# Hash-masked attention before two gated layers: split q and k in place, three fills a head, one matmul for the shift row

## Chip, cores and metric

One core of a Trainium2 chip runs the whole program in one launch. The metric is device time in microseconds. A profiled execution gives a span (first to last instruction of the program) and a time that is a little longer; the times of plain runs compare with the latter.

## The reference, cut to what matters

```python
# q, k, v: (2, 8, 768, 64); proj: (64, 6)
q_bucket = sum(((q @ proj) > 0) * 2 ** arange(6))          # k_bucket alike
mask = q_bucket[:, :, :, None] == k_bucket[:, :, None, :]
scores = where(mask, q @ k.T / 8, -1e9)
attn = exp(scores - max(scores)); attn = attn / (sum(attn) + 1e-9)
x = (attn @ v) as (2, 768, 512)                            # heads side by side
# layer 1: gate = sigmoid(causal 5-tap convolution of x), per channel
x = (gate * (x @ w_val)) @ w_out
# layer 2: token shift, xk and xr are mixes of x and the row before it
k = relu(xk @ w_k); y = (k * k) @ w_v
out = sigmoid(xr @ w_r) * y
```

## The kernel before

**Numbers in two halves.** Products keep float32 accuracy by splitting each factor into a high half (rounded to the matmul type) and the rest (low half). Keys lie along partitions in the score matmuls: a head's q tile and k tile have 128 partitions and two planes of 768 columns. In `scores` (L329, L330) the first matmul multiplies plane 1 and the second plane 0, both over 128 partitions, into one PSUM bank of 128 keys by 384 queries. Plane 0 holds 64 rows of the high half and a block of 32 rows that makes the mask: bits of the hash, which give a large negative number where q and k fall into different buckets, and one row with the negative row maximum of each query (the shift). Plane 1 holds cross terms of high and low halves.

**Before smax and scores.** Heads go in pairs. `load_q` and `load_k` fetch a pair, `turn` transposes on TensorE into PSUM, `turn_out` (ACT) copies to `t32`. `split_hi` (L445, ACT) writes the rounded half of a pair to `hlq` or `hlk`, `split_lo` (L449, VectorE) the rest. Then `fill` moves each head's halves from there to the head's tiles by four transfers on SP's queue (L468 and L470 of 384 KB, L472 and L474 of 192 KB), and `penalty` (L479, L482) moves the bits of `bits_gt` and `bits_big` there, both heads of a pair in one transfer of 96 KB. The tiles of two pairs take turns, in the memory named `big`.

**A head.** `smax` (L355) computes plane 0 products of a block of 128 queries with all keys, `smax_row` (L359, VectorE) takes the maximum, `smax_all` (L363) negates it. `shift` (L368) turns the six columns of maxima into a row: six matmuls with a one-column factor, each of 128 columns. `shift_row` (L374, ACT) copies that row of 768 to its place in plane 0. Then per block of 128 keys and half of the queries: `scores`, `exp` (L334, ACT) into a ring of 11 buffers, `add` (L338, GpSimd) for the sums, and `values` (L343, four matmuls for a block of keys). `sums`, `sums_fold` (L391, a small transfer to `dn`), `spread`, `spread_out` (L406, a small transfer to `rb`) and `norm` (L410) give the quotient, and `norm_out` writes the head to `xT`.

**Weights.** Each of 28 weight tiles is loaded (`weight`, L600), converted in two passes on ACT (L583, L586) and two on VectorE (L590, L594), and split by `part_hi` (ACT) and `part_lo` (VectorE for a list of tiles, else GpSimd). The order is val, out, k, r, v: 20 tiles have memory of their own, and the eight of v pass through three late buffers. The gated layers (all matmuls L648) run in four chunks of 384 tokens; the first ones begin between the last heads.

**Order.** The program text has a hand-over list, `ORDER`: some 2300 events such as `sc201` (`scores`, head 2, block 0, half 1), which fixes the order on every engine and on SP's queue at once. Each engine works its own instructions strictly in this order. All transfers of this stage are issued by SP in this order; before it issues one, SP waits for what the transfer reads and overwrites.

Of the kernel before, what the change touches and what calls it, by code (L numbers as in the profile page):

```python
# [11 lines left out]
R = mybir.dt.float32r  # L12
# [8 lines left out]
NRING = 11  # L21
# [23 lines left out]
fl ze00 ze01 ft01 ft00 fy01 fh01 lv0 ve0 fy00 lq10 lk1 lq11 we00 ve1 fc fb00 fb01 fz00 fz01 fb11 fg wa0 ft10 wa2 wa8  # L45
wa7 ft11 fy11 fb10 fz10 fy10 sb fh10 fh00 wa4 fh11 ve2 sm00 fz11 sr00 sm01 fo00 fo01 sx sr01 sz se0 fo02 fo03 sm02
tu100 sr02 sm03 to100 sr03 sm04 se1 fo10 wa5 sa003 tu101 sr04 fo11 sm05 to101 lq21 sr05 hi10 tu110 lq20 sh003 hr003
fo12 to110 fo13 ze10 ze11 sm10 sr10 sc000 sm11 tu111 sa036 ex000 sm12 to111 sr11 sc010 wa6 hi11 lo10 fi20 fi30 we10
sh036 ex010 hr036 lo11 bi1 ad010 fi22 sc001 sm13 bg1 fi21 ex001 sr12 bb1 sc011 fi32 tu200 sr13 sc020 pe100 ex011 sm14
ex020 pe101 sc021 sr14 ad020 sc030 pe111 ex021 sm15 to200 sc031 ad011 lk2 sr15 wa3 ex031 wa9 pe110 ex030 ad021 sa106  # L50
sc041 sc040 ad030 ex041 fi23 sh106 ex040 hr106 ad031 sc050 sc051 ex050 tu201 fi33 ad041 ex051 sc100 sc101 ad040 lq31
ex100 wa1 ex101 fi31 sc110 we01 ad050 sc111 lq30 ex110 sm20 we03 sm21 ex111 ad110 sc120 sr21 sc121 ex120 va00 we02
# [744 lines left out]
```

## Time and profile before

| | us |
|---|---|
| median of 3 runs | 503.97 (502.52 to 504.17) |
| profiled execution | 503.95 |
| its span | 502.2 |
| TensorE busy | 475.0 |
| VectorE busy | 331.5 |
| ACT busy | 315.9 |
| GpSimd busy | 191.9 |

TensorE's busy time is the union of its matmuls from issue to end. Matmuls overlap in the pipe, so the time that one adds to a row of others is less than its duration. The start of the program (loading, first pair) takes some 26 us, the attention lasts until about 260 us, and the rest belongs to the gated layers. PEclk is the granted share of TensorE's full clock.

### The profile page before, as it was taken

What the parts mean: (1) busy time and instruction counts of PE and PEld (TensorE: products, weight loads), DVE (VectorE), ACT (ScalarE), POOL (GpSimd) and SP (SyncE); (2) the same over time, 40 slices, a digit from 0 to 9 for tenths busy, and PEclk for the clock granted to TensorE, in tenths of its full rate; (3) what the DMA queues carried; (4) which work ended last, traced back from release to release, by engine and by line L of the source; (5) the groups of instructions that cost most, each with busy time, mean ns of one, the idle gap of its engine ahead of it and who ended that gap; (6) DMA issues with size and microseconds to landing.
All of it is one profiled execution on the core that took longest, in us unless ns stands there. A gap on an engine that the chain in (4) does not pass through costs nothing.

```text
span 502.2 us, 7241 instructions
## 1 busy us (share of the span) xinstructions
PE 475.0 (95%) x2545; PEld 366.5 (73%) x2545; DVE 331.5 (66%) x522; ACT 315.9 (63%) x638; POOL 191.9 (38%) x216
## 2 busy tenths in 40 slices
PE   4899999999997998999899899999999999999997
PEld 2566575656664665656477799989998999988985
DVE  0676777685976586899848997769634774335222
ACT  3688777688775775878797668665426543344121
POOL 4488567657664746877555142120000000000000
PEclk9999999999999998999899899999999999999999
DMA  7199687788669985730121102200100010000101
GB/s 180 52 222 216 147 235 173 192 210 190 180 173 211 175 176 123 168 116 2 44 85 43 44 0 85 85 1 0 64 0 2 0 43 22 1 0 1 63 1 63
DMA packets 43523, 47.57 MB, mean 95 GB/s; under 512 B 29251, under 2 KB 33887, under 8 KB 43487
## 3 DMA queue, kind: packets, MB, share of 16 engines
q1 hardware_dynamic: 43486, 47.12, 38.7%
q8 instruction: 20, 0.33, 0.3%
q14 instruction: 17, 0.13, 0.1%
HBM read 24.35 MB, written 3.15 MB: 55 GB/s over the span
## 4 chain that ended last, share of the span: by engine, by line
PE 72%; ACT 8%; DVE 7%; DMA 6%; SPq 2%; issue 2%; ACTq 0%; DVEq 0%
PE bank L648 27%; PE smb L648 16%; PE bank L343 9%; PE bank L329 6%; PE bank L330 5%; PE smb L355 5%; DMA big<-hlk 3%; DVE mx L359 2%; ACT ring L334 2%; DVE gp L676 1%; PE bank L383 1%; DMA big<-hlq 1%; DMA rb<-rhl 1%; PE bank L438 1%; PE bank L453 1%
## 5 line engine op out<-in xcount | busy, mean ns | idle before, releaser
L338 POOL TENSOR_TENSOR acc<-acc,ring 128x384 f32<-128x384 f32 x128 | 115.1, 920 | 28.6 <-ACT ring L334 25.9
L334 ACT ACTIVATE ring<-bank 128x384 f32<-128x384 f32 x192 | 87.9, 490 | 33.2 <-PE bank L330 29.2
L359 DVE TENSOR_REDUCE mx<-smb 128x1 f32<-128x768 f32 x96 | 88.5, 950 | 24.5 <-PE smb L355 23.6
L329 PE MATMUL bank<-big,big 128*128 128x384 f32 x192 | 72.6, 378 | 6.7 <-ACT ring L334 6.5
L648 PE MATMUL bank<-big,wlo 128*128 128x384 f32 x224 | 75.7, 338 | 0.0
L343 PE MATMUL bank<-ring,vn 128*64 128x385 f32 x384 | 71.5, 506 | 0.0
L330 PE MATMUL bank<-big,big 128*128 128x384 f32 x192 | 65.6, 342 | 0.5 <-ACT big L374 0.5
L648 PE MATMUL bank<-big,wk 128*128 128x384 f32 x256 | 65.3, 336 | 0.0
L648 PE MATMUL smb<-wv,kk 128*128 128x512 f32 x176 | 62.6, 392 | 0.0
L329 PEld LDWEIGHTS bank<-big,big 128*128 128x128 f32 x192 | 36.4, 189 | 30.9 <-ACT ring L334 24.3
L355 PE MATMUL smb<-big,big 128*128 128x384 f32 x192 | 50.4, 356 | 4.8 <-DMA big<-hlk 2.3
L338 POOL TENSOR_TENSOR acc<-ring 128x384 f32<-128x384 f32 x32 | 35.7, 1128 | 45.0 <-ACT ring L334 42.6
L343 PEld LDWEIGHTS bank<-ring,vn 128*64 128x64 f32 x384 | 25.0, 139 | 32.1 <-issue 30.5
L648 PEld LDWEIGHTS bank<-big,wk 128*128 128x128 f32 x256 | 46.5, 188 | 2.4
L676 DVE SCALAR_TENSOR_TENSOR gp<-xT,vec,gp 128x384 f32<-128x384 f32 x64 | 41.6, 670 | 3.5 <-ACT gp L674 3.2
L648 PEld LDWEIGHTS bank<-big,wlo 128*128 128x128 f32 x224 | 42.5, 190 | 0.0
L355 PEld LDWEIGHTS smb<-big,big 128*128 128x128 f32 x192 | 32.8, 190 | 12.6 <-issue 6.4
L729 DVE TENSOR_TENSOR kk<-gp,kk 128x384 fp32r<-128x384 f32 x32 | 17.8, 563 | 31.5 <-ACT kk L727 31.5
L648 PEld LDWEIGHTS smb<-wv,kk 128*128 128x128 f32 x176 | 33.0, 188 | 6.0
L330 PEld LDWEIGHTS bank<-big,big 128*128 128x128 f32 x192 | 36.5, 190 | 0.9 <-ACT big L374 0.7
L648 PE MATMUL smb<-lo,kk 128*128 128x512 f32 x88 | 34.6, 393 | 0.0
L725 DVE TENSOR_TENSOR gp<-gp,bank 128x384 f32<-128x384 f32 x32 | 17.4, 551 | 25.2 <-ACT gp L723 25.1
(135 smaller groups left out, 822.0 us busy)
## 6 DMA issues: line engine op xcount, KB each, us to landing
big<-hlq SPq DMA_DIRECT2D x14, 384.0 KB
big<-hlk SPq DMA_DIRECT2D x14, 384.0 KB
raw<-in_moe_w_k_dram SPq DMA_DIRECT2D x8, 512.0 KB
raw<-in_moe_w_v_dram SPq DMA_DIRECT2D x8, 512.0 KB
vn<-in_v_dram SPq DMA_DIRECT2D x8, 384.0 KB
out_dram<-rs SPq DMA_DIRECT2D x12, 256.0 KB
qn<-in_q_dram SPq DMA_DIRECT2D x14, 192.0 KB
kn<-in_k_dram SPq DMA_DIRECT2D x7, 384.0 KB
```

What stands on the lines that cost most here:

```text
L329: nc.tensor.matmul(out=st, lhsT=kd[:, 1, col(t)], rhs=qd[:, 1, half(hf)], start=True, stop=False)
L330: nc.tensor.matmul(out=st, lhsT=kd[:, 0, col(t)], rhs=qd[:, 0, half(hf)], start=False, stop=True)
L334: nc.scalar.activation(out=probs(n, t, hf)[:, 0:HF], in_=st, func=AF.Exp, scale=scale)
L338: nc.gpsimd.tensor_add(acc, probs(n, 0, hf)[:, 0:HF] if t == 1 else acc, probs(n, t, hf)[:, 0:HF])
L343: nc.tensor.matmul(out=bank[PV_BANK][64 * hf:64 * hf + 64, 0:HF + 1], lhsT=tl[:, n % 2, t, :], rhs=probs(n, t, hf)[:, 0:HF + 1], start=t = ...
L355: nc.tensor.matmul(out=sm[:, hf, 0:HF], lhsT=qd[:, 0, col(t)], rhs=kd[:, 0, half(hf)], start=True, stop=True)
L359: nc.vector.tensor_reduce(out=mxs[n % 2][:, t, 0:1], in_=smb[(7 * n + t) % 2][:, :, 0:HF], op=ALU.max, axis=AX.XY)
L383: nc.tensor.matmul(out=tp[o:o + 32], lhsT=ones, rhs=acc_b[m % 3][hf], start=True, stop=True)
L648: nc.tensor.matmul(out=ps, lhsT=w[a], rhs=xx[c], start=first and m == 0, stop=last and m == 2)
L676: nc.vector.scalar_tensor_tensor(out=gp, in0=src, scalar=w, in1=gp, op0=ALU.mult, op1=ALU.add)
L725: nc.vector.tensor_mul(rl, rl, mm(j, "k", f))
L729: nc.vector.tensor_sub(kk[:, 1], rl, f32(kk[:, 0]))
```

## The change

- The high halves are written straight into the head's tiles by ACT (`split_hi`, now per head), at partitions 0 to 63 or 64 to 127 by the parity of the head, and k's low half likewise by VectorE; only q's low half has a buffer of its own (`qlo`).
- `fill` has three transfers of 192 KB a head: q's high half and k's high half to plane 1, and q's low half.
- `penalty` moves one head at a time (eight transfers of 48 KB a pair).
- For heads 1 to 15 `shift` is one matmul with the six columns of maxima as its factor; ACT copies the 6 x 128 result to `shr`, and a new transfer, `shift_fold` (`hd`), lays it out as a row of 768 in plane 0.
- k and v are loaded a head at a time, with queries' order of tokens (runs of 256 bytes).
- The weights' order is val, out, k, v, r; the tiles of v and r go through the late buffers.
- The ring of exponentials has 13 buffers.
- `ORDER` is new throughout, with 2385 events for 2329.

```diff
-NRING = 11
+NRING = 13
-LO_DVE = (0, 1, 2, 3, 4, 5, 6, 7, 18, 19)
-WINDOW = 93376
+LO_DVE = (0, 1, 2, 3, 4, 5, 6, 7, 16, 17)
+WINDOW = 101568
 ORDER = """
-fl ze00 ze01 ft01 ft00 fy01 fh01 lv0 ve0 fy00 lq10 lk1 lq11 we00 ve1 fc fb00 fb01 fz00 fz01 fb11 fg wa0 ft10 wa2 wa8
...
+ve0 wa0 ze00 fl wa2 wa8 ze01 ft00 wa7 fy00 ft01 fc lq10 fb00 fb01 fy01 lq11 ve1 fz00 fh01 lk10 fz01 fb10 we00 ft10
...
+lo210 fi42 bb2 sh206 su1 va04 hr206 we14 sy1 hd2 lo200 hi201 ve3 we30 sm30 hi211 ve4 sm31 pe2100 tu300 sr30 fi50 va05
+to300 fi41 tu301 lo211 vo0 sc201 pe2000 to301 sc200 we23 sm32 pe2110 ex200 sr31 tu310 ex201 pe2101 sc210 sr32 sc211
...
+scf11 ta022 sud exf11 ta023 exf10 vl013 vod weg3 adf10 ta014 scf20 scf21 exf20 adf11 vl000 exf21 ta004 vl001 syd sg01
+vl002 sfd adf20 scf30 ta032 vl003 exf30 vl020 sg00 adf30 ta033 scf40 scf31 adf21 sue exf31 ga000 vae0 sye ga010 exf40
+vae1 ta034 ph7 adf40 ta024 vae2 xs110 weg2 vae3 adf31 ga011 spd vae4 sfe sg03 vae5 ga001 sod pl7 scf41 ga002 voe vl021
+weg4 ta100 vaf0 exf41 xs111 wei0 pha ga012 adf41 vaf1 spe ta110 vaf2 ph8 noc ph9 ta101 pl8 scf50 vl022 nnc exf50 scf51
+sg02 ou000 exf51 pl9 vl023 xs130 phb vl100 xs131 xs120 nod adf50 vl030 soe nnd vl031 adf51 vl032 vl033 ta102 pla suf
...
+    shr = sb("shr", 128, dtype=R)
-    w_tiles = [(n, c, o) for n in ("val", "out", "k", "r", "v") for o in range(w_all[n].shape[1] // WC)
+    w_tiles = [(n, c, o) for n in ("val", "out", "k", "v", "r") for o in range(w_all[n].shape[1] // WC)
-    NEARLY = NW - KF
+    NEARLY = NW - KF - KC
-    hls = {"q": wtile("hlq", 2, S, dtype=R), "k": wtile("hlk", 2, S, dtype=R)}
+    qlo = wtile("qlo", S, dtype=R)
+    def rows_of(h, part, size=64):
+        o = 64 * ((h + part) % 2)
+        return slice(o, o + size)
     def shift(n, a, b):
-        for x in range(a, b):
-            nc.tensor.matmul(out=smb[(7 * n + NT) % 2][0:1, x // TH, col(x % TH)], lhsT=mxr[n % 2][:, x:x + 1],
-                             rhs=identr, start=True, stop=True)
+        sm = smb[(7 * n + NT) % 2]
+        if n == 0:
+            ...
+        else:
+            nc.tensor.matmul(out=sm[0:NT, 0, 0:128], lhsT=mxr[n % 2], rhs=identr, start=True, stop=True)
     def shift_row(n, a, b):
-        row = head(n)[0][0:1, 0].rearrange("r (h c) -> r h c", c=HF)
-        hs = slice(a // TH, b // TH)
-        nc.scalar.copy(row[:, hs], smb[(7 * n + NT) % 2][0:1, hs, 0:HF])
+        if n == 0:
+            ...
+        else:
+            nc.scalar.copy(shr[0:NT], sm[0:NT, 0, 0:128])
+    def shift_fold(n):
+        nc.sync.dma_start(out=f32(head(n)[0][rows_of(n, 1, 1), 0]), in_=f32(shr[0:NT]))
-    def load_k(i):
+    def load_k(i, x):
         b, h = divmod(2 * i, H)
-        nc.sync.dma_start(out=kn,
-                          in_=k[b, h:h + 2].rearrange("h (p t) d -> p t h d", t=NT))
+        nc.sync.dma_start(out=kn[:, :, x], in_=k[b, h + x].rearrange("(t p) d -> p t d", t=NT))
-    def split_hi(i, x):
-        nc.scalar.copy(hls["qk"[x]][:, 0], t32s[x])
-    def split_lo(i, x):
-        h = hls["qk"[x]]
-        nc.vector.tensor_sub(h[:, 1], t32s[x], f32(h[:, 0]))
+    def split_hi(i, x, h):
+        if x == 0:
+            nc.scalar.copy(qs[i % 2][:, h, 0], t32s[0])
+        else:
+            rows = rows_of(h, 0)
+            nc.scalar.copy(ks[i % 2][rows, h, 0], t32s[1][rows])
+    def split_lo(i, x, h):
+        if x == 0:
+            nc.vector.tensor_sub(qlo, t32s[0], f32(qs[i % 2][:, 0, 0]))
+        else:
+            rows, kd = rows_of(h, 0), ks[i % 2][:, h]
+            nc.vector.tensor_sub(kd[rows, 1], t32s[1][rows], f32(kd[rows, 0]))
     def fill(n, part):
         qd, kd = head(n)
-        rows = slice(64 * (n % 2), 64 * (n % 2) + 64)
+        rows, over = rows_of(n, 0), rows_of(n, 1)
         if part == 0:
-            nc.sync.dma_start(out=f32(qd[64:128]), in_=f32(hls["q"][rows, 0:1]).to_broadcast((64, 2, S)))
+            nc.sync.dma_start(out=f32(qd[rows, 1]), in_=f32(qd[rows, 0]))
         elif part == 1:
-            nc.sync.dma_start(out=f32(kd[64:128]), in_=f32(hls["k"][rows]))
-        elif part == 2:
-            nc.sync.dma_start(out=f32(qd[0:64, 1]), in_=f32(hls["q"][rows, 1]))
-        else:
-            nc.sync.dma_start(out=f32(kd[0:64, 1]), in_=f32(hls["k"][rows, 0]))
+            nc.sync.dma_start(out=f32(qd[over, 1]), in_=f32(qlo[rows]))
+        else:
+            nc.sync.dma_start(out=f32(kd[over, 1]), in_=f32(kd[rows, 0]))
-    def penalty(i, hf, x):
+    def penalty(i, hf, x, h):
+        tl, r = (qs, ks)[x][i % 2], 32 * hf + 64 * (1 - x)
+        nc.sync.dma_start(out=f32(tl[rows_of(h, 1, KB), h, 0, half(hf)]), in_=f32(bits[r:r + KB, h * x]))
...
```

## Rows read from the trace of the kernel before

**Rows 1.** The page's busy line (engine, us, share, instructions) and chain by engine.

```profile
PE 475.0 (95%) x2545; PEld 366.5 (73%) x2545; DVE 331.5 (66%) x522; ACT 315.9 (63%) x638; POOL 191.9 (38%) x216
...
PE 72%; ACT 8%; DVE 7%; DMA 6%; SPq 2%; issue 2%; ACTq 0%; DVEq 0%
```

**Rows 2.** Table of stretches: each engine's busy us, PEclk, DMA share, GB/s.

```profile
160.00:180.00 20.00, 20.00 (x114) 11.95 (x116) 11.59 (x15) 13.50 (x31) 14.19 (x16) 0.91 0.90 176
180.00:200.00 20.00, 17.72 (x99) 11.57 (x95) 14.84 (x21) 13.57 (x29) 9.90 (x12) 0.91 0.68 139
...
240.00:260.00 20.00, 17.52 (x92) 12.08 (x93) 13.94 (x25) 17.79 (x30) 10.13 (x9) 0.91 0.26 81
...
320.00:340.00 20.00, 20.00 (x101) 17.81 (x100) 13.99 (x25) 13.49 (x27) 4.31 (x3) 1.00 0.01 4
```

**Rows 3.** Chain of waits, 150 to 215 us: start, us, what (transfers).

```profile
153.13 6.76 DMA big<-hlk
...
184.36 10.52 DMA big<-hlk
...
207.16 6.01 DMA big<-hlq
```

**Rows 4.** Timeline of TensorE: start, us, line, matmul [idle before, releaser].

```profile
159.93 0.44 PE L329 MATMUL bank<-big,big 128*128 128x384 f32 x1 [2.18 <-ACT ring L334]
...
195.02 0.58 PE L355 MATMUL smb<-big,big 128*128 128x384 f32 x2 [2.28 <-DMA big<-hlk]
```

**Rows 5.** Chain of waits again, 166 to 183 us: TensorE's pieces.

```profile
166.00 0.45 PE smb L368 x6
...
173.44 0.33 PE bank L438 x3
173.76 0.80 PE bank L343 x4
...
175.04 0.35 PE smb L355 x2
175.38 0.18 PE bank L329
...
181.08 1.44 PE bank L343 x8
182.53 0.37 PE bank L410
```

**Rows 6.** Groups of instructions: line, engine, tile, count, busy us, mean ns, idle before.

```profile
L586 ACT ACTIVATE raw<-raw 128x512 int32<-128x512 uint32 x28 | 22.8, 818 | 0.0
L594 DVE CUSTOM_DVE_ANT_0 w<-raw,w 128x1024 uint16<-128x1024 uint16 x20 | 17.0, 856 | 3.6 <-ACT raw L586 3.5
L374 ACT CAST big<-smb 1x768 fp32r<-1x768 f32 x15 | 11.7, 782 | 4.2 <-PE smb L368 4.1
L449 DVE TENSOR_TENSOR hlk<-t,hlk 128x768 fp32r<-128x768 f32 x7 | 8.2, 1176 | 7.6 <-ACT hlk L445 7.6
L445 ACT CAST hlq<-t 128x768 fp32r<-128x768 f32 x7 | 5.9, 838 | 0.3 <-DMA big<-hlq 0.2
L679 ACT ACT_TABLE_LOAD x4 | 5.1, 1283 | 0.1
```

**Rows 7.** The page's DMA queue: packets, MB, share of 16 engines over the span.

```profile
q1 hardware_dynamic: 43486, 47.12, 38.7%
```

**Rows 8.** Timeline of SP and VectorE: issue of two small transfers, start of their readers.

```profile
117.87 0.61 SPq L391 DMA_DIRECT2D dn<-acc  x1
120.04 0.23 DVE L396 RECIPROCAL rec<-dn 128x12 f32<-128x12 f32 x1 [0.40 <-DMA dn<-acc]
...
143.11 0.60 SPq L391 DMA_DIRECT2D dn<-acc  x1
146.34 0.23 DVE L396 RECIPROCAL rec<-dn 128x12 f32<-128x12 f32 x1 [0.59 <-DMA dn<-acc]
```

**Rows 9.** Waits of TensorE: who for whom, us in total, times, longest.

```profile
PE bank L329 <- ACT ring L334: 6.5, 8, 2.5
```

More of the change, by code (lines that the diff above doesn't have):

```diff
@@ L254, in fused_kernel @@
     t32s = [wtile("t32", S) for x in range(2)]
-    hls = {"q": wtile("hlq", 2, S, dtype=R), "k": wtile("hlk", 2, S, dtype=R)}
+    qlo = wtile("qlo", S, dtype=R)
     bits = wtile("bits", 2, HF, dtype=R)
-    raw_t = [wtile("raw", WC, 2, dtype=I32) for n in range(2)]
+    wtile("free", FREE)
+    raw_t = [wtile("raw", WC, 2, dtype=I32) for n in range(NRAW)]
     ring = [wtile("ring", 2, RSTEP) for n in range(NRING)]
@@ L366, in shift @@
     def shift(n, a, b):
-        for x in range(a, b):
-            nc.tensor.matmul(out=smb[(7 * n + NT) % 2][0:1, x // TH, col(x % TH)], lhsT=mxr[n % 2][:, x:x + 1],
-                             rhs=identr, start=True, stop=True)
-    def shift_row(n, a, b):
-        row = head(n)[0][0:1, 0].rearrange("r (h c) -> r h c", c=HF)
-        hs = slice(a // TH, b // TH)
-        nc.scalar.copy(row[:, hs], smb[(7 * n + NT) % 2][0:1, hs, 0:HF])
+        sm = smb[(7 * n + NT) % 2]
+        if n == 0:
+            for x in range(a, b):
+                nc.tensor.matmul(out=sm[0:1, x // TH, col(x % TH)], lhsT=mxr[0][:, x:x + 1], rhs=identr,
+                                 start=True, stop=True)
+        else:
+            nc.tensor.matmul(out=sm[0:NT, 0, 0:128], lhsT=mxr[n % 2], rhs=identr, start=True, stop=True)
+    def shift_row(n, a, b):
+        sm = smb[(7 * n + NT) % 2]
+        if n == 0:
+            row = head(0)[0][rows_of(0, 1, 1), 0].rearrange("r (h c) -> r h c", c=HF)
+            hs = slice(a // TH, b // TH)
+            nc.scalar.copy(row[:, hs], sm[0:1, hs, 0:HF])
+        else:
+            nc.scalar.copy(shr[0:NT], sm[0:NT, 0, 0:128])
+    def shift_fold(n):
+        nc.sync.dma_start(out=f32(head(n)[0][rows_of(n, 1, 1), 0]), in_=f32(shr[0:NT]))
     def pair_of(n):
@@ L499, in zero @@
     def zero(pair, x):
-        nc.gpsimd.memset(f32((ks, qs)[x][pair][KB:64, :, 0]), 0.0)
+        for h in range(2):
+            o = 64 * (1 - h) + KB
+            nc.gpsimd.memset(f32((ks, qs)[x][pair][o:o + KB, h, 0]), 0.0)
     def first_const():
@@ L574, in first_lo @@
         elif part == 2:
-            for y, hi in enumerate((q1, q0[:, 0])):
+            for y, hi in ((x, q0[:, 0]), (1 - x, q1)):
                 nc.gpsimd.tensor_sub(odd_even(q1, y), by_slot(first_half(x, 1)[64 * y:64 * y + 64]),
@@ L596, in weight @@
     def weight(i, part):
[L597 removed]
+        raw, dst = raw_t[i % NRAW], w32[w_tiles[i]]
         if part == 0:
@@ L755, in fused_kernel @@
     todo = {f.__name__: f for f in (
-        scores, exp, add, values, zero, values_out, smax, smax_row, smax_all, shift, shift_row, sums, sums_copy,
+        scores, exp, add, values, zero, values_out, smax, smax_row, smax_all, shift, shift_row, shift_fold, sums, sums_copy,
         sums_fold, spread, spread_out, norm, norm_out, load_q, load_k, load_v, turn, turn_out, split_hi,
```

270 lines of the change are left out of this document (132 added, 138 removed).

## The prediction

> **What bounds the kernel now.** I read the page's busy line and its chain first [rows 1]: TensorE is busy 475.0 of 502.2 us and carries 72% of the chain that ended last, ACT 8%, VectorE 7%, DMA 6%. So time is gained in two ways only: less TensorE work, or fewer moments in which TensorE stands still. The busy figure hides part of the second kind, since a matmul that waits while it is in the pipe counts as busy. Next comes the table of stretches [rows 2]. From about 300 us on (320:340 stands for it) TensorE is busy 20.00 of 20 with DMA at 1%: the two gated layers at the end are plain TensorE work, and no transfer matters there. Up to 200 us the DMA engines are 0.68 to 0.90 busy, and two stretches, 160:180 and 180:200, have a granted clock of 0.91: part of them ran at 1.2 GHz in place of 2.4. The timeline of TensorE shows why [rows 4]: it had been idle for 2.18 us before 159.93 and 2.28 us before 195.02. The chain of waits says on what [rows 3]: it goes through a fill of 6.76 us from 153.13 and one of 10.52 us from 184.36, both `big<-hlk`, and a third of 6.01 us from 207.16. The timeline names ACT for the first of these gaps and a fill for the second; the chain names a fill for both, and since scores wait for several things at once, I believe the chain. So the fills are what stops TensorE twice, while elsewhere in the attention it makes many short stops, mostly for the exponentials [rows 9].
>
> **The change part by part.** All sums are made against the profiled execution: span 502.2 us, 503.95 us with what lies around it; the median of the runs shown is 503.97, so no correction is needed between them.
>
> Shift rows. Six one-column matmuls took 0.45 us in a row [rows 5]; five go for 15 heads. 5/6 of 0.45 is 0.375, times 15 is 5.6 us. Part of a run is the change of shape before it, which the one matmul that stays still pays, and not every stretch is TensorE-bound: I take 4.0, bounds 3.0 to 5.6.
>
> Fills. Before, a head had four: twice 384 KB and twice 192 KB, 1152 KB; now it has three of 192 KB, 576 KB. Over 14 heads 8.26 MB leave a queue that moved 47.12 MB in 38.7% of the span [rows 7]. That is 194 us of DMA time, 4.1 us for a MB, so 34 us less, in the stage that was 0.68 to 0.90 busy [rows 2]. In addition smax no longer reads anything that a fill wrote: the high halves are written in place by ACT, and smax waits for ACT and the penalties alone, so the wait of 2.28 us [rows 4] loses its cause. What I count is the two idle times, 2.18 + 2.28 = 4.5 us, and the low clock behind them: two stretches of 20 us at 0.91 lost 2 x 20 x 0.09 = 3.6 us [rows 2, 4]. Sum 8.1, taken as 8.0. The third wait ended on ACT and stays uncounted. Bounds 4 (the idle time turns into the next wait, only the clock comes back) to 12 (the third wait and smaller ones too); the three pieces together are 23 us [rows 3], but TensorE worked under most of that.
>
> Number of transfers. The penalties become 56 of 48 KB for 28 of 96 KB, k and v loads 15 more, folds 15 new, fills 14 fewer: 44 more issues of 0.6 us on SP's queue [rows 8], 26 us over the attention's 250 us. SP's own issuing carries 2% of the chain, 10 us [rows 1]; a tenth more of SP's time makes that some 1 us, which I cost at nothing. What a fuller queue would make late is the fold (below), and its price is there. The Trainium skill, page "DMA: Bandwidth & Descriptors", section "Rules for kernel authors", speaks against this part: it wants small transfers joined, and says that under 64 KB one mostly pays overhead. By it the 28 added penalties would each cost as much as a 96 KB one, 0.4 us at 4.1 us for a MB, 11 us in all, a third of the 34 us saved; the fill term would be 5.4 in place of 8.0 and the time 498.2. No row before shows a 48 KB penalty beside such traffic.
>
> The fold. This is the new wait on the path. The row of maxima went from PSUM to its place by one ACT copy of 782 ns [rows 6]; now a short ACT copy of 6 x 128 is followed by a 3 KB transfer on SP's queue, and the head's first scores wait for its landing. The nearest rows are the small `dn` transfers, from issue to the start of their reader: 2.17 us (117.87 to 120.04) and 3.23 us (143.11 to 146.34) [rows 8]. Queued behind the waiting matmul is everything on TensorE; behind the fold's own wait for ACT on SP stand the next fills, penalties and loads. What covers it is the TensorE work that the new order puts between the fold and the first scores: for head 2, two smax (0.35 each), two turns (0.33 each) and one values step (0.64) are 2.0 us [rows 5]. Counted alike, the 15 folds have 1.7, 2.0, 2.7, 2.1, 2.1, 3.4, 2.0, 2.4, 2.6, 3.5, 2.1, 2.4, 1.9, 1.9 and 2.5 us of cover. With a landing of 2.4 us, nearer to the lighter row since the DMA load falls, the shortfalls add up to 3.4 us; with 2.2 us to 1.8; with 3.1 us to 11.9; with 3.5 us to 17.3. I take +3.4, bounds 0 to 17.
>
> ACT and VectorE. Splitting in place needs 14 more copies of 838 ns on ACT, +11.7 us, and 7 more subtractions of some 1.18 us on VectorE, +8.2 us [rows 6]. The shift row's copy shrinks; a sixth of the columns makes it some 0.25 us (an estimate between 0 and 0.78), 15 x 0.53 = 8 us less. Each r weight tile passes ACT three times and VectorE twice or three times; at the listed 818 and 856 ns as upper prices, four tiles take at most 9.8 and 6.8 us out of the attention [rows 6]. Net: ACT up to 6 us less, VectorE about 1 us more. In 160:200 ACT was busy 13.5 of 20 and VectorE 11.6 and 14.8 [rows 2]; that idle time hides it, so 0 there (1 us if it didn't). But r's tiles were converted late in the attention, where in 240:260 ACT was busy 17.79 of 20 and TensorE lost 2.5 us [rows 2]. There I count -2.0, bounds 0 to -4. The same work lands in a stage with ACT at 13.49 of 20 under a full TensorE [rows 2]: hidden, 0 (up to +4 if v or r tiles come late).
>
> The order. Values steps are written in 42 runs on TensorE in place of 35. Entering a run costs 0.16 us (x4 takes 0.80, x8 1.44: 0.64 for four, 0.16 over) and leaving it 0.19 (a 384-column matmul after it 0.37, in a row 0.18) [rows 5]; 7 x 0.35 = +2.5, bounds 0 to 2.5. In the last head exponentials and sigmoids alternate nine times in place of seven; each change loads an ACT table, 1283 ns [rows 6]. That is 2.6 us on ACT just where TensorE waits for it; half lands: +1.3, bounds 0 to 2.6. At the start three small vector loads now stand ahead of the first q and k loads on SP: at most 3 x 0.6 [rows 8], while warm-up matmuls move ahead; +0.5, bounds -1 to +1.8. With a ring of 13 where the order uses 11 at most, some of the 6.5 us of open waits of scores for the exponentials [rows 9] should go; 2.18 of these are counted already, of the other 4.3 I take -2.0, bounds 0 to -4.3.
>
> Sum: -4.0 -8.0 +3.4 -2.0 +2.5 +1.3 +0.5 -2.0 = -8.3; 503.95 - 8.3 = 495.6.
>
> **The rivals.** Slower: the fold is late. Place: the first scores of heads 1 to 15. Price: without the fold the sum is 492.2, so it decides at 11.8 us, which is a landing of 3.1 us by the list above; at 3.5 us the time is 509.5. For it speak 3.23 us in one of the two rows, and that SP issues in order, so that one blocked transfer ahead delays the fold [rows 8]. Against it: the DMA load falls by about a sixth, and the lighter row is the better picture of it.
>
> About the same: the stops for fills were hidden anyway, and the waits for exponentials take their place [rows 9]; the fill term is 0, and the time 503.6. For it speaks that the timeline named ACT before 159.93; against it, that the clock was low in just these two stretches.
>
> Larger gain: no fold shows, and the small fill waits go too: -5 -12 +0 -3 +2.5 +1.3 +0.5 -2 = -17.7, 486.2.
>
> Late weights: v and r tiles arrive after their turn in the first chunk of the gated layers and take back most: about +5 on the forecast, 501.
>
> That the change doesn't do what it says is hardly possible for bytes and matmul counts, both are in the code.
>
> **How the numbers follow.** Forecast 0.47 (its own range 491 to 500), larger gain 0.18, about the same 0.17, late fold 0.13, late weights 0.05. The range of 8 in 10 is 486 to 505: it leaves out the late fold past its turning point and the far end of the larger gain. What can be told from no change is about 0.3%, 1.5 us: faster 0.47 + 0.18 + 0.05 + 0.03 of the middle case = 0.73, same 0.11, slower 0.13 + 0.03 = 0.16.
>
> **What the changed profile would show.** Fills: `big<-big` and `big<-qlo` of 192 KB, DMA share in 40:200 near 0.65, no transfer of over 5 us in the chain, no stretch below full clock in 150:200. Shift: 21 matmuls for 96 (15 single ones and the six of head 0). Fold: waits of a score's second matmul, which reads the row (before, L330), on the transfer `big<-shr`, together some 3 us; over 10 would be the late fold. Tables: nine loads in the last head. I would be wrong if TensorE's short stops for exponentials grow by as much as the long ones shrink, or if the gated layers start at the same time and end later.

## The result, and the profile after

The kernel after takes 486.86 us (486.02 to 487.87), the kernel before 503.66 beside it: 0.967 of the time, interval 0.964 to 0.970, a gain of 16.8 us. In a later measurement on another chip (`after_again`, below) it was 0.971 (0.968 to 0.974), 14 us. The forecast was 495.6, a gain of 8.3; the result is that of the rival called larger gain, 486.2. That rival met the time and not the terms, so its agreement is in part luck: its 12 us for the fills and 3 for r's weights did not come, and the gains from ACT's copy and the start are not in it.

From the page of the kernel after: the busy line, the chain by engine, and the DMA queue; they answer to [rows 1] and [rows 7].

```profile
PE 465.5 (96%) x2470; PEld 357.8 (74%) x2470; DVE 337.7 (69%) x529; ACT 318.9 (66%) x654; POOL 192.6 (40%) x220
...
PE 83%; ACT 9%; DVE 5%; DMA 2%; issue 1%; POOL 0%; SPq 0%; ACTq 0%; POOLq 0%
...
q1 hardware_dynamic: 51298, 38.91, 30.5%
```

DMA has fallen from 6% of the chain to 2% (0% in `after_again`), SP's issuing from 2% to nothing, and TensorE carries 83% for 72%. 8.2 MB are gone from the queue, as worked out. The table of stretches of the kernel after, in the stretches of [rows 2] (busy us of TensorE, weight loads, VectorE, ACT, GpSimd; then PEclk, DMA share, GB/s):

```profile
160.00:180.00 20.00, 19.55 (x108) 12.78 (x104) 15.74 (x23) 16.34 (x38) 14.12 (x16) 1.00 0.54 144
180.00:200.00 20.00, 19.43 (x109) 11.18 (x107) 18.29 (x25) 16.48 (x35) 12.53 (x13) 1.00 0.45 108
240.00:260.00 20.00, 15.68 (x76) 10.55 (x77) 13.81 (x24) 14.96 (x28) 9.24 (x8) 0.91 0.09 27
```

In 160 to 200 (the first two) the granted clock is 1.00 for 0.91, with DMA at about half. What is left of low clock is in 240 to 260, at the attention's end.

TensorE's waits for the exponentials, after's answer to [rows 9] (us in total, times, longest), and the group of the short ACT copy that takes the place of L374 in [rows 6]:

```profile
PE bank L339 <- ACT ring L344: 3.5, 8, 1.7
```

```profile
L392 ACT CAST shr<-smb 6x128 fp32r<-6x128 f32 x15 | 3.8, 250 | 6.1 <-PE smb L383 4.4 <-issue 1.2 <-ACT ring L344 0.5
```

These waits fell from 6.5 us, of which 2.18 are the first stop of [rows 4], to 3.5 (4.1 in `after_again`). The copy takes 250 ns, as estimated, for 782: 8.0 us of ACT over 15 heads.

Where the time went is read best from the first score matmul of each head (first `L329` before, first `L339` after), in us from the start:

| | head 0 | head 1 | head 9 | head 12 | head 15 | last score | end |
|---|---|---|---|---|---|---|---|
| before | 26.1 | 38.3 | 149.1 | 198.9 | 237.0 | 258.4 | 502.2 |
| after | 19.6 | 34.7 | 142.4 | 182.4 | 221.5 | 244.0 | 486.1 |
| difference | -6.5 | -3.6 | -6.7 | -16.5 | -15.5 | -14.4 | -16.1 |

So there are a gain ahead of head 1, which the prediction's start term has with the other sign, a steady one of 0.4 us a head, which is about what the shift's matmuls and ACT copy are worth (below), the large one between heads 9 and 12 where the two stops stood, and a loss of 2.1 us from head 12 to the last score. The gated layers add little.

### The profile page after: what moved, and what is told of

It reads as the page before. It is cut to its first block, busy times and chain, and to the rows that moved or that the text cites. A ratio compares the mean times of both kernels' runs of the same rounds, so it can differ in the third digit from the quotient of the medians.

```text
span 486.1 us, 7152 instructions
## 1 busy us (share of the span) xinstructions
PE 465.5 (96%) x2470; PEld 357.8 (74%) x2470; DVE 337.7 (69%) x529; ACT 318.9 (66%) x654; POOL 192.6 (40%) x220
## 3 DMA queue, kind: packets, MB, share of 16 engines
q1 hardware_dynamic: 51298, 38.91, 30.5%
## 4 chain that ended last, share of the span: by engine, by line
PE 83%; ACT 9%; DVE 5%; DMA 2%; issue 1%; POOL 0%; SPq 0%; ACTq 0%; POOLq 0%
PE bank L675 27%; PE smb L675 17%; PE bank L353 12%; PE bank L339 8%; PE smb L365 6%; PE bank L340 6%; PE bank L462 2%; ACT ring L344 2%; PE bank L404 2%; DVE mx L369 1%; DMA big<-bits 1%; PE bank L536 1%; ACT L706 1%; DVE gp L703 1%; PE bank L483 1%
## 5 line engine op out<-in xcount | busy, mean ns | idle before, releaser
L348 POOL TENSOR_TENSOR acc<-acc,ring 128x384 f32<-128x384 f32 x128 | 119.0, 951 | 27.2 <-ACT ring L344 25.0
L339 PE MATMUL bank<-big,big 128*128 128x384 f32 x192 | 73.4, 382 | 3.8 <-ACT ring L344 3.5
L353 PE MATMUL bank<-ring,vn 128*64 128x385 f32 x384 | 73.1, 508 | 2.3 <-ACT vm L358 2.3
L340 PE MATMUL bank<-big,big 128*128 128x384 f32 x192 | 64.9, 338 | 0.7 <-ACT big L390 0.7
L675 PE MATMUL smb<-wv,kk 128*128 128x512 f32 x176 | 61.4, 391 | 0.0
L339 PEld LDWEIGHTS bank<-big,big 128*128 128x128 f32 x192 | 35.9, 187 | 29.2 <-ACT ring L344 18.8
L348 POOL TENSOR_TENSOR acc<-ring 128x384 f32<-128x384 f32 x32 | 33.7, 1071 | 45.5 <-ACT ring L344 41.0
L365 PE MATMUL smb<-big,big 128*128 128x384 f32 x192 | 49.1, 351 | 0.4 <-DVE mx L369 0.2
L703 DVE SCALAR_TENSOR_TENSOR gp<-xT,vec,gp 128x384 f32<-128x384 f32 x64 | 43.4, 695 | 1.0 <-ACT gp L701 0.4
L754 ACT CAST kk<-gp 128x384 fp32r<-128x384 f32 x32 | 16.2, 512 | 32.1 <-PE smb L675 31.6
L340 PEld LDWEIGHTS bank<-big,big 128*128 128x128 f32 x192 | 36.3, 189 | 1.0 <-ACT big L390 1.0
```

Source lines behind the costliest of these rows:

```text
L339: nc.tensor.matmul(out=st, lhsT=kd[:, 1, col(t)], rhs=qd[:, 1, half(hf)], start=True, stop=False)
L340: nc.tensor.matmul(out=st, lhsT=kd[:, 0, col(t)], rhs=qd[:, 0, half(hf)], start=False, stop=True)
L348: nc.gpsimd.tensor_add(acc, probs(n, 0, hf)[:, 0:HF] if t == 1 else acc, probs(n, t, hf)[:, 0:HF])
L353: nc.tensor.matmul(out=bank[PV_BANK][64 * hf:64 * hf + 64, 0:HF + 1], lhsT=tl[:, n % 2, t, :], rhs=probs(n, t, hf)[:, 0:HF + 1], start=t = ...
L365: nc.tensor.matmul(out=sm[:, hf, 0:HF], lhsT=qd[:, 0, col(t)], rhs=kd[:, 0, half(hf)], start=True, stop=True)
L675: nc.tensor.matmul(out=ps, lhsT=w[a], rhs=xx[c], start=first and m == 0, stop=last and m == 2)
```

## The experiments

All ratios are to the kernel before on the same chip, and spans are those of the profiled execution. Variants of after are compared by span with its two profiled executions, 486.1 and 486.3 us; by ratio with 0.967 and 0.971. The four executions of after in the result have spans of 484.2 to 486.1 us, so a difference of 2 us by span alone shows little.

| kernel | median us | ratio (interval) | span |
|---|---|---|---|
| before_warm_first | 499.14 | 0.993 (0.990 to 0.997) | 499.4 |
| after_warm_late | 492.05 | 0.980 (0.975 to 0.985) | 491.5 |
| before_less_fill | 498.41 | 0.993 (0.989 to 0.996) | 495.7 |
| before_conv_later | 505.56 | 1.004 (1.000 to 1.008) | 505.1 |
| before_conv_less_fill | 498.74 | 0.991 (0.988 to 0.995) | 500.0 |
| before_no_fill | 493.98 | 0.981 (0.978 to 0.984) | 491.9 |
| after_fill_bytes | 499.39 | 0.995 (0.992 to 0.998) | 494.6 |
| after_two_folds | 500.11 | 0.994 (0.991 to 0.996) | 497.7 |
| after_five_more | 490.74 | 0.976 (0.972 to 0.979) | 488.5 |
| after_row_copy | 493.63 | 0.980 (0.977 to 0.983) | 491.9 |
| after_shift_six | 495.47 | 0.985 (0.980 to 0.990) | 493.9 |
| after_less_split | 488.85 | 0.973 (0.969 to 0.977) | 487.7 |
| after_split_pool | 490.28 | 0.976 (0.972 to 0.981) | 487.6 |
| after_one_switch | 484.61 | 0.965 (0.961 to 0.968) | 483.5 |
| after_pool_switch | 489.47 | 0.975 (0.971 to 0.979) | 488.5 |
| after_again | 488.15 | 0.971 (0.968 to 0.974) | 486.3 |
| after_five_loads | 482.71 | 0.961 (0.958 to 0.964) | 480.7 |

**The start.** The warm-up matmuls (`wa`) were moved to after's places in before, and to before's places in after.

```diff
 before_warm_first: ORDER of before
-fl ze00 ze01 ft01 ft00 ... fb11 fg wa0 ft10 wa2 wa8 wa7 ft11
+wa0 fl wa2 wa8 ze00 ze01 ft01 wa7 ft00 ... fb11 fg ft10 ft11
 after_warm_late: ORDER of after
-ve0 wa0 ze00 fl wa2 wa8 ze01 ft00 wa7 fy00 ... fh00 fg lk11 fb11 ft11
+ve0 ze00 fl ze01 ft00 fy00 ... fh00 fg wa0 lk11 fb11 wa2 wa8 wa7 ft11
```

> The kernel before with one edit: the four warm-up events of the start stand ahead of and between the first transposes (as in the changed kernel) and no longer between the pair's first and second half, where they took TensorE from 11.30 to 15.14 us. Theory A (the start's gain of 4.6 us, seen at head 1's first scores, is these matmuls off the path and the full clock at 7 in place of 14.7 us): the first scores come 3 to 6 us earlier than at 26.1, the full clock starts at about 7 us, and the time falls by 3 to 5 us to 499 to 501. Theory B (the gain at the start comes from the order of the other first steps): first scores within 1 us of before, time within 1.5 us of 503.7.

> The changed kernel with the four warm-up events back at the places of the kernel before (behind the first penalties, ahead of the last of the four transposes). Theory A: the first scores come 3 to 6 us later than at 19.6 and the time rises by 3 to 5 us to 490 to 492. Theory B: within 1.5 us of 486.9.

Timeline of TensorE, kernel before: the warm-ups (L510) stand between transposes (L524) that are needed.

```profile
9.89 1.48 PE L536 MATMUL smb<-t,pd 64*32 64x384 f32 x2 [1.22 <-DVE big L540]
11.30 1.22 PE L510 MATMUL bank<-ident 128*128 128x128 f32 x4
12.32 0.85 PE L524 MATMUL bank<-ident,vn 128*128 128x128 f32 x3
12.96 2.35 PE L510 MATMUL bank<-ident 128*128 128x128 f32 x12
15.14 0.49 PE L524 MATMUL bank<-ident,vn 128*128 128x128 f32 x3
```

The same in the kernel after (warm-ups L536, transposes L550):

```profile
1.56 2.93 PE L536 MATMUL bank<-ident 128*128 128x128 f32 x12 [1.56 <-POOL ident masks.py:199]
4.46 0.90 PE L550 MATMUL bank<-ident,vn 128*128 128x128 f32 x3
...
8.66 0.80 PE L562 MATMUL smb<-t,pd 64*32 64x384 f32 x2 [0.80 <-DVE big L566]
```

In after the twelve run while the first load is still under way and end 0.3 us behind the point where before's first transposes could start (4.17 us), so they cost next to nothing; before, they ran in a gap that a transpose could have had. The same two matmuls for the hash took 1.48 us before and 0.80 after, too: the trace's first record of a granted clock of 1.00 is at 14.7 us before and at 7.3 after, and at 7.6 and 16.6 in the two variants. So both edits move the places and the clock together, and no run tells the two apart. Moved in before, the first scores of head 1 came at 33.9 for 38.3 us, 4.4 earlier, and 2.8 of it remained at the end; moved back in after, head 1 came at 39.9 and the span grew by 5.3. The places of the warm-ups are worth 3 to 5 us. The rest of the new start cost some of it: without the early warm-ups after's head 1 comes at 39.9, 1.6 us later than before's 38.3.

**The stops between heads 9 and 12.** Four kernels take parts of the load or of the order out of before.

```diff
 before_less_fill (before_no_fill: every part)
 def fill(n, part):
+    if n >= 4 and part >= 2:
+        return
 before_conv_later: ORDER of before (before_conv_less_fill: both edits)
-... wea1 ... wea2 wea3 ... sca31 wea4
+... sca31 wea1 wea2 wea3 wea4
```

> The kernel before without its third and fourth fill for heads 4 to 15 (24 transfers of 192 KB), so these heads multiply stale low halves; smax still waits for the two large fills of 384 KB. Theory C (bytes): the two large fills land in 4 to 6 us, both long stops go, time down by 5 to 8 us to 496 to 499. Theory D (the wait of smax and scores for a large fill as such): at least one stop of over 1.5 us on a fill stays and the time falls by less than 3 us.

> The kernel before, with three steps of one weight tile (the two ACT conversions and the VectorE shift of the k weight whose raw load landed at 158.8 us) written 75 places later in the order, behind the first scores of head 10; nothing is left out. Theory W (the first stop, 2.2 us before 159.93, is ACT standing in order behind a weight load that lands late, as the timeline says): the stop and the stretch of low clock after it go, 3 us less, about 499.5 beside 502.3. Theory F (the stop is the fill big<-hlk, as the chain of waits says): the stop stays at 159 to 160 us and the time is that of before, within 1 us.

> Both edits on the kernel before: the weight tile's conversion moved as in before_conv_later, and the low halves of q and k (fills 2 and 3) left out for heads 4 to 15, whose scores then read old low halves. If a full queue has two ways to stop TensorE in before, one through ACT and one through a fill, then both low clocks are gone and the lag between heads 9 and 12 falls by 7 us: 495 to 496 beside 502.3. If the first stop only needs fewer bytes, or has yet another transfer behind it, the time is that of before_less_fill, 498.4.

> The kernel before without the four fills of heads 4 to 15 (the scores of these heads read old halves): the bytes go, and with them what waits for a fill: scores, and the staging copies on ACT that write over what a fill still reads. Theory F (both stops between heads 9 and 12 are what full queues do, directly or through ACT, which stands in order): no low clock between 150 and 200 us, the lag from head 9 to 12 grows by 5 us as in after in place of 12.3, 495 or less beside 502.5. Rival (the weight load that ACT waited for at 158.8 us is late without the fills too): the first stop stays, 498.5 as without fills 2 and 3.

Without fills 2 and 3 the second stop of [rows 4] went; the first stayed and grew to 3.18 us, behind ACT, which waited 3.66 for its weight tile. TensorE in `before_less_fill`:

```profile
158.93 0.45 PE L329 MATMUL bank<-big,big 128*128 128x384 f32 x1 [3.18 <-ACT ring L334]
```

What ACT did in the kernel before, timeline of ACT around the first stop (start, us, line, what, and the idle time before it with its releaser):

```profile
155.30 0.88 ACT L334 ACTIVATE ring<-bank 128x384 f32<-128x384 f32 x2 [0.53 <-PE bank L330]
158.83 0.66 ACT L583 ACTIVATE w<-raw 128x512 f32<-128x512 f32 x1 [2.66 <-DMA raw<-in_moe_w_k_dram]
159.40 0.86 ACT L334 ACTIVATE ring<-bank 128x384 f32<-128x384 f32 x2
```

So ACT stood for 2.66 us in front of a weight tile that had not landed, the exponentials queued behind it came at 159.40, and the scores that need their ring buffers at 159.93. ACT as the timeline names it was right. But moving this conversion away freed nothing. Timelines of ACT and TensorE in `before_conv_later`, and then in `before_conv_less_fill`:

```profile
165.10 0.83 ACT L445 CAST hlk<-t 128x768 fp32r<-128x768 f32 x1 [7.08 <-DMA vn<-in_v_dram]
166.75 0.69 PE L329 MATMUL bank<-big,big 128*128 128x384 f32 x1 [4.21 <-ACT ring L334]
```

```profile
164.16 0.83 ACT L445 CAST hlk<-t 128x768 fp32r<-128x768 f32 x1 [5.03 <-DMA big<-hlk]
165.81 0.69 PE L329 MATMUL bank<-big,big 128*128 128x384 f32 x1 [2.15 <-ACT ring L334]
```

The next in ACT's order is the copy into `hlk`, and it must not overwrite what a fill still reads from there; it waited 7.08 and 5.03 us, and TensorE 4.21 and 2.15 behind it. (The first line's releaser is a load of v; among transfers, only fills read the buffer.) Only without any fill are both stops gone; ACT's wait for the weight tile, and the table of stretches, of `before_no_fill`:

```profile
154.92 0.67 ACT L585 ACTIVATE w<-raw 128x512 f32<-128x512 f32 x1 [0.55 <-DMA raw<-in_moe_w_k_dram]
```

```profile
160.00:180.00 20.00, 20.00 (x128) 13.12 (x125) 14.12 (x21) 14.93 (x34) 12.24 (x15) 1.00 0.27 78
180.00:200.00 20.00, 19.69 (x115) 13.09 (x113) 18.43 (x25) 17.89 (x37) 18.41 (x20) 1.00 0.20 63
```

Heads 9 to 12 took 41.7 us there, 49.8 in before and 40.0 in after, and the time fell by 9.4 us. So the load on the queue makes the stops, through several waiters: a score, a weight tile, a staging copy. The change halves the fills' bytes and takes away the staging copy of k; the DMA share in 160 to 200 fell from 0.90 and 0.68 to 0.54 and 0.45.

**The same bytes in after.** Each fill of heads 2 to 13 is issued twice, first into memory that nothing reads.

```diff
 def fill(n, part):
+    if n < 14:
+        src = (qd[rows, 0], qlo[rows], kd[rows, 0])[part]
+        nc.sync.dma_start(out=spare[rows, S * part:S * part + S], in_=f32(src))
```

> The changed kernel with every fill of heads 2 to 13 issued twice, the first time into a buffer that nobody reads: 36 more transfers of 192 KB, so the bytes of four fills a head are back, but smax and scores wait for nothing more than in the changed kernel. Theory C (the two long stops came from full DMA queues, so from bytes): DMA share back at about 0.8 in 40:200, long fills in the chain, time up by 5 to 9 us to 492 to 496. Theory D (they came from smax waiting for a large fill): time up by less than 2.5 us, though the DMA share rises as much.

45.99 MB on the queue, near before's 47.12, cost 8.4 us of span and 2.4 to 2.8% of the time; the profiled execution lies at the low end of its kernel's times (496.33 beside a median of 499.39), so its 8.4 is a low value. Heads 9 to 12 took 45.9 us: 6 of the 10 us gained there come back with the bytes. The bytes are worth about what the fill term says, or more. Half of the 8.4 is new, though. Waits of TensorE, and then a piece of the chain of waits, in `after_fill_bytes`:

```profile
PE bank L340 <- DMA big<-shr: 4.3, 4, 2.2
```

```profile
127.06 5.70 DMA big<-shr
132.76 0.04 issue
132.80 0.44 PE bank L340
```

The fold is issued on the same queue, and this one took 5.70 us where the DMA share was 0.92 (120 to 140 us). In after TensorE's list of waits has no entry for it: from its issue to its semaphore the 15 folds took 1.81 to 2.17 us, median 1.83. Here the median is 2.14 and the longest 5.70. With before's load the late fold, the rival on the slow side, is real.

**The fold's price.** The row goes through a second buffer in heads 1 to 13.

```diff
 def shift_fold(n):
+    nc.sync.dma_start(out=f32(spare[0:NT, 0:128]), in_=f32(shr[0:NT]))       # n < 14
-    nc.sync.dma_start(out=..., in_=f32(shr[0:NT]))
+    nc.sync.dma_start(out=..., in_=f32(spare[0:NT, 0:128]))
```

> The kernel after, with the row of maxima of heads 1 to 13 sent through a second buffer, so that two 3 KB transfers follow one another: some 3.7 to 4 us from the ACT copy to the landing in place of 1.85. Nothing is left out. By the prediction's list of covers (1.7 to 3.5 us) a landing of 3.7 us falls short by 17 us over these 13 heads: about 503. If the cover in the running kernel is longer than the counted TensorE work, it costs under 5 us: 487 to 491.

Chain of waits in `after_two_folds`, the two transfers of one head, and TensorE's list of waits:

```profile
148.19 1.90 DMA free<-shr
150.15 1.97 DMA big<-free
```

```profile
PE bank L340 <- DMA big<-free: 6.8, 10, 1.4
```

It costs 11.5 us of span and 2.3 to 2.7% of the time, but only 6.8 of that are waits for the fold; another 3.5 are waits for penalties (1.8) and `rb` (1.7) which after lacks or has at 0.2. The list of covers gives 17 us at a landing of 3.7. It was too strict, and the profile of after shows by how much. Timelines of SP and TensorE for head 13, whose measured cover is the shortest (1.9 in the list):

```profile
194.51 0.74 SPq L395 DMA_DIRECT2D big<-shr  x1
196.78 0.44 PE L339 MATMUL bank<-big,big 128*128 128x384 f32 x1
197.06 0.34 PE L340 MATMUL bank<-big,big 128*128 128x384 f32 x1
```

From the fold's issue to the matmul that reads the row (L340) it is 2.54 us here, and 2.54 to 4.11 in the 15 heads, 0.5 to 1.5 more than listed in each. With these covers a landing of 3.7 us falls short by 6.9 us in heads 1 to 13, which is the 6.8 measured, and the forecast's 2.4 by nothing. So by the measured covers the fold would have been free at 2.4 too; its landing at 1.83 only added room.

**The shift rows, in parts.** One kernel has before's shift in full (six matmuls, one long ACT copy, no fold), one only before's number of matmuls, one only a second ACT copy as long as before's.

```diff
 after_five_more: def shift(n, a, b), heads 1 to 15
+    for x in range(1, NT):
+        nc.tensor.matmul(out=sm[0:1, x // TH, col(x % TH)], lhsT=mxr[n % 2][:, x:x + 1], rhs=identr, ...)
 after_row_copy: def shift_row(n, a, b), heads 1 to 13
     nc.scalar.copy(shr[0:NT], sm[0:NT, 0, 0:128])
+    nc.scalar.copy(spare[0:1, 0:S]..., sm[0:1, 0:2, 0:HF])
 after_shift_six: shift, shift_row
-    if n == 0:
+    if True:
 def shift_fold(n):
+    return
```

> The kernel after, with the shift rows of all 16 heads by six one-column matmuls and one ACT copy of the whole row, as before, and without the 3 KB folds; nothing else is changed. By the prediction's own working the matmuls cost 15 x 0.375 = 5.6 us at most, some 4 on the path (3.0 to 5.6), and without the fold 0 comes back, since TensorE waited 0 for it in after: 490 to 492 beside 486.9 for after. Rival: the saved matmuls were hidden in other short stops, then within 1 us of after. A rival on the other side: the fold does cost, though no wait shows it, then under 487.

> The kernel after, with five one-column matmuls ahead of the single shift matmul of heads 1 to 15, their results not read: TensorE's work of before, with after's short ACT copy and fold; nothing is left out. By the prediction 4.0 us (3.0 to 5.6) slower than after: 490 to 492.5. If all of after_shift_six's loss of 8.6 us is TensorE's work: 494 to 496. With after_row_copy it should add up to some 8.6 us.

> The kernel after, with one more ACT copy in heads 1 to 13, right behind the short copy of the shift rows: 1 x 768 out of PSUM, as before's copy of the row (782 ns), into a buffer that nothing reads; 10.2 us of ACT work. TensorE's work and the folds stay as they are. Theory P (after_shift_six lost 8.6 us since the long row copy holds up ACT, which the prediction booked at nothing): 3 to 5 us slower than after, 490 to 492. Theory Q (the prediction: ACT's idle time hides it, all of the loss is TensorE's own work): within 1 us of 486.9.

By span the five matmuls cost 2.3 us (2 to 4.3 by the ratios), the copy 5.7 (4.4 to 6.6), and all of it 7.7. So the prediction's 4.0 for the matmuls was right or a little high, and its zero for ACT was the larger mistake: 10.2 us of ACT cost up to 5.7. What stands behind the copy shows in ACT's timeline of `after_row_copy`:

```profile
101.66 0.24 ACT L392 CAST shr<-smb 6x128 fp32r<-6x128 f32 x1
101.81 0.78 ACT L394 COPY free<-smb 1x768 f32<-1x768 f32 x1
102.50 0.98 ACT L612 ACTIVATE w<-raw 128x512 f32<-128x512 f32 x1
103.39 1.65 ACT L615 ACTIVATE raw<-raw 128x512 int32<-128x512 uint32 x2
```

The copy stands at a head's boundary, in a row of ACT work, and ahead of the last exponentials of one head or the first of the next. Compared matmul by matmul with after, nearly all of the added delay arises within 5 us of a shift matmul, half of it in front of scores (L339). But a third of it, 1.9 us, is one stop behind GpSimd. TensorE's stop in `after_row_copy`, and all additions of exponentials on GpSimd there (shortest, median and longest in ns):

```profile
48.85 0.84 PE L406 MATMUL bank<-acc,ones 128*32 128x384 f32 x4 [1.70 <-POOL acc L348]
L348 POOL TENSOR_TENSOR acc<-acc,ring x128: 853/865/3121, 28.5 to 255.4; 128x384 f32<-128x384 f32 x128
```

One addition, from 45.68 us, took 3.12 us. The same stop stands at 48 to 50 us in `after_shift_six` and in `after_less_split` (below), which has less ACT work than after and not more; in after the longest addition took 1.68. Without this stop the copy's price is 3.8 us for 10.2, 0.37 for each, and with it 0.56; no run tells whether the copy brings the stop about.

**Is ACT dear everywhere?** The ACT copy of k's high halves was left out for 12 heads, or put on GpSimd.

```diff
 def split_hi(i, x, h):                                  # the k branch
-    nc.scalar.copy(ks[i % 2][rows, h, 0], t32s[1][rows])
+    if 2 * i + h < 4:                                   # after_less_split
+        nc.scalar.copy(ks[i % 2][rows, h, 0], t32s[1][rows])
+    nc.gpsimd.tensor_copy(ks[i % 2][rows, h, 0], t32s[1][rows])     # after_split_pool
```

> The kernel after without the ACT copy of k's high halves (64 x 768, 828 ns) for heads 4 to 15, 12 copies, 9.9 us of ACT; their scores read old high halves. VectorE's subtractions, the fills and all else stay. Theory P (a us of ACT in the attention costs some 0.65 us, as in after_row_copy): 6 us faster than after, about 480.5. Theory Q (only the place behind the shift rows is dear, ACT's time elsewhere is hidden): within 1.5 us of 486.9.

> The kernel after with k's 14 high-half copies on GpSimd in place of ACT; nothing is left out. By theory P 11.6 us less on ACT are worth up to 7 us, less what the copy costs in GpSimd's order behind the additions of the exponentials (951 ns each, GpSimd busy 0.67 of the stage): 481 to 486. Rival: the copies come late there, VectorE's subtraction and with it its maxima wait, and it is slower than after, 488 to 495. By theory Q within 1.5 us of 486.9.

No. Without 9.9 us of these copies it was no faster (span 1.5 longer, after a stop of 2.05 us at 48 us that after lacks, the one of `after_row_copy`); from head 2 to head 15 it gained 1.0 us on after. So these added copies cost 1 us at most, next to nothing, as the prediction had it. On GpSimd the time came 0.5 to 0.9% longer, with an interval that touches that of `after_again`.

**The tail.** Sigmoids of the gated layer's first chunk stand between the last head's exponentials.

```diff
 after_one_switch: ORDER of after, fourteen events, in their order
-... sg01 ... sg00 ... ga000 ... ga010 ... ga011 ... sg03 ... ga001 ... ga002 ... ga012 ... sg02 ou000 exf51
+... exf51 sg01 sg00 ga000 ga010 ga011 sg03 ga001 ga002 ta100 ga012 ta110 ta101 sg02 ou000
 after_five_loads: ORDER of after
-syd sg01 vl002 ... vl020 sg00 ... scf51 sg02 ou000 exf51
+syd vl002 ... vl020 sg01 sg00 ... scf51 exf51 sg02 ou000
```

> The kernel after with 14 steps of the gated layer's first chunk (its sigmoids and the first products) written behind the last exponential, so that ACT changes its table two times at the attention's end in place of nine; seven loads of 1.28 us are 9 us less on ACT there, where TensorE stops for 1.7, 2.3 and 3.3 us. If these loads set the attention's tail: 3 to 6 us faster, 481 to 484. If TensorE then lacks the moved products in the tail, or the sigmoids come late for the gated layer: no change or up to 3 us slower.

> Both edits on the kernel after, the k copies on GpSimd and the sigmoids behind the last exponential; nothing is left out. If both gain by themselves and lie in different stages (before and after 225 us), their gains add up: 476 to 481. If either loses, the sum of the two.

> The kernel after, unchanged, as the measure for the variants on the same chip: 0.967 of before's time, within 0.003.

> The kernel after with one sigmoid written beside the next one and one behind the last exponential; the products stay in the tail (one only follows its sigmoid). ACT changes its table five times at the attention's end in place of nine, 4 x 1.28 = 5.1 us less. If the loads set the tail and TensorE's 5.3 us stop in after_one_switch came from the products that were moved: 3 to 5 us faster than after_again. If it came from the sigmoids' lateness: 0 to 2 us.

Timeline of TensorE in the kernel after, its stops behind 226 us:

```profile
231.69 0.44 PE L339 MATMUL bank<-big,big 128*128 128x384 f32 x1 [1.69 <-ACT ring L344]
240.80 2.16 PE L353 MATMUL bank<-ring,vn 128*64 128x385 f32 x12 [2.26 <-ACT vm L358]
...
252.19 0.84 PE L404 MATMUL bank<-acc,ones 128*32 128x384 f32 x4 [3.27 <-DVE xT L437]
```

The same in `after_five_loads`:

```profile
238.99 3.86 PE L353 MATMUL bank<-ring,vn 128*64 128x385 f32 x12 [2.42 <-ACT vm L358]
249.28 0.84 PE L404 MATMUL bank<-acc,ones 128*32 128x384 f32 x4 [0.96 <-DVE xT L437]
```

The same in `after_one_switch`:

```profile
245.26 1.28 PE L675 MATMUL smb<-big,wout 128*128 128x384 f32 x2 [5.25 <-ACT big L717]
```

Four table loads fewer, 5.1 us of ACT, gave 5.4 us beside `after_again`, with intervals that do not touch: 1.35 us for a load, its full time. It arises at the end: the last score starts at 244.0 us in after and in `after_five_loads`, and most of the gain comes between 248 and 257 us, where the stop for `xT` fell from 3.27 to 0.96. With all sigmoids behind the last exponential TensorE, whose next products hang on them, stops once for 5.25 us, and half of the gain is lost (2.8 us by span, for 5.6). `after_five_loads`, at 0.961, is faster than both kernels. `after_pool_switch` was no faster than `after_split_pool` by more than their intervals, so the gains did not add up as expected.

## Why the prediction came out short, step by step

| term | forecast us | measured us | by |
|---|---|---|---|
| shift matmuls | -4.0 | -2 to -4 | after_five_more |
| shift row's ACT copy | 0 | -3 to -4.5 (estimate) | after_row_copy, at 0.37 to 0.56 us for each us |
| fills, bytes | -8.0 | -7 to -9 | heads 9 to 12, before_no_fill |
| fold | +3.4 | 0 | no wait in the profile after |
| start, warm-ups | +0.5 | -3 to -5 | before_warm_first, after_warm_late |
| tables | +1.3 | some +2.7 (estimate) | two loads at the 1.35 us of after_five_loads |
| r weights, values runs, order | -1.5 | not taken apart | |

**Mis-sized: the start.** The prediction priced the vector loads on SP and put the warm-ups at next to nothing, with -1 as its bound. That the warm-ups stood between needed transposes for 1.22 and 2.35 us stands in TensorE's timeline of the first 26 us, which the argument left out. This step has the wrong sign; its error is 3.5 to 5.5 us, beside 3.4 for the fold and 3 to 4.5 for ACT's copy.

**Mis-sized: the fold, by its covers above all.** The choice of 2.4 us lay near the lighter of [rows 8]; these rows measure from the issue to the reader's start, in a fuller queue. 1.83 us was measured with the lighter load. The larger mistake is the list of covers: every head has 0.5 to 1.5 us more between the issue and the reader than the TensorE work that was counted, and with the measured covers 2.4 us costs nothing and 3.1 us, the rival's turning point, 1.8 in place of 11.9. What fills the difference was not taken apart; a part is the score's first matmul (L339), which stands ahead of the reader and does not read the row, 0.28 us in head 13. Fills and fold were added up as two terms, but the fold's landing hangs on the load of the fills: with before's load it cost 4.3 us, with after's none.

**Mis-sized: ACT's copy.** The prediction had the copy shrink by 8 us in all and took its price from ACT's idle share in 160 to 200. A share over 20 us doesn't say what stands behind an instruction; at 0.37 to 0.56 us for each us these 8 us are 3 to 4.5. For the split copies, elsewhere in ACT's order, the same reasoning held.

**Right in size, wrong in mechanism: the fills.** 8.0 was forecast, and 7 to 9 came, with the clock back at 1.00. But "smax no longer reads what a fill wrote" explains the second stop alone. For the first I believed the chain, which named the fill, against the timeline, which named ACT. ACT was the one that TensorE waited for, and ACT itself waited for transfers. Both views were links of one chain, since the queue served the fill and the weight tile at once: without any fill ACT's wait for that tile was 0.55 us for 2.66, and the stop was gone.

**Right: shift, tables' direction, no late weights.** 21 shift matmuls took the place of 96, 15 of 128 x 6 and the six of head 0. TensorE's list of waits has no entry for a weight tile, so the rival of late weights did not come true. Nine table loads are there, as counted; in the tail a load cost all of its time, not half. The rival called about the same fell with the fills.

**Not taken apart: r's weights, the order, the ring.** The -2.0 for r's weights should show late in the attention, where after lost 2.1 us from head 12 to the last score; the two added table loads lie there too, and no run separates them. The ring's -2.0 came as -0.8 at best: the open waits for exponentials went from 4.3 to 3.5 us, and to 4.1 in `after_again`.

**The rule on small transfers.** By the Trainium skill, "DMA: Bandwidth & Descriptors", section "Rules for kernel authors", 56 penalties of 48 KB should have cost more for a MB than 28 of 96 KB. For a single transfer the trace agrees: from issue to its last semaphore update a 96 KB penalty took 3.04 us in the median before, and a 48 KB one 2.33 after, though under a lighter load (those behind 40 us). But the fill term did not shrink to the 5.4 that the prediction worked out by it, and the whole queue's time fell: 30.5% of 486.1 us for 38.91 MB is 3.8 us for a MB, and it was 4.1 [rows 7], with 18% more packets. That figure mixes all transfers, and no run isolates what the smaller penalties cost.

The measured terms sum to about -12 to -20, the kernel gained 14 to 17. They are not independent: of the 6.5 us at head 0 3.6 were left at head 1, and the values runs' cost was not isolated.

## What to carry to other kernels

Price an edit by what stands behind it in its engine's order at that place, not by the engine's idle share: one ACT copy cost 0.37 to 0.56 us for each us at a head's boundary, another, elsewhere in ACT's order, next to nothing. Count what covers a transfer on the path from its issue to the instruction that reads it, and not only the work that you know of: here the list was 0.5 to 1.5 us short in each head. Small transfers are as late as the queue they share, so a term for bytes and a term for a small transfer on the path belong into one sum. And read the first microseconds and the last stage's table loads as closely as the middle: both were worth 3 to 5 us here.

## What the runs showed of the hardware

A 3 KB transfer between two places of on-chip memory took 1.75 to 2 us from issue to semaphore in nearly all cases, under a DMA share of 0.45 to 0.70 (stretches of 20 us, 40 to 200), two in a row mostly 3.6 to 3.8; with 18% more bytes (0.47 to 0.92) the median was 2.14 and the longest 5.70. In two places the traces show VectorE and GpSimd at work at once and the one that began later taking longer; why, no run here shows. In `after_row_copy` a GpSimd addition that began at 45.68 us, 0.02 behind a row of three VectorE instructions, took 3.12 us for the usual 0.87. In the kernel after the addition began at 46.00, and it was VectorE's subtraction, 0.01 behind, that took 1.67 us, where in `after_row_copy` the same one took 0.94:

```profile
46.01 1.67 DVE L479 TENSOR_TENSOR big<-t,big 64x768 fp32r<-64x768 f32 x1
```

An ACT table load took 1283 ns every time, and at the attention's end four of them were worth 5.4 us of the kernel's time. ACT's timeline in the kernel after shows ACT at work right up to a load, and the next instruction right behind it:

```profile
227.50 0.50 ACT L408 ACTIVATE acc<-bank 128x384 f32<-128x384 f32 x1
228.01 1.28 ACT L706 ACT_TABLE_LOAD   x1
229.31 0.53 ACT L706 ACTIVATE gp<-gp 128x384 f32<-128x384 f32 x1
229.85 1.28 ACT L344 ACT_TABLE_LOAD   x1
```

The Trainium skill, "ScalarE: Activation LUTs", section "What ACT_TABLE_LOAD costs", counts 2.66 us for a change, half of it a drain; these rows show no such second half, and the measured price of a load, 5.4 / 4 = 1.35 us, has no room for it.
